# First batch of a gated recurrence: row maxima of chunks 0 and 1 spread from three 16-bit parts, and VectorE's scans placed ahead of a column copy

## The chip, the cores and the metric

One core of one Trainium2 chip. Its engines are TensorE (PE, with its weight loads PEld), VectorE (DVE), ScalarE (ACT), GpSimd (POOL) and SyncE (SP), which issues all transfers here. The metric is the time on the device in microseconds, as the median of several runs; beside it stands one execution taken by the hardware profiler.

## What is computed

Two blocks in a row. The first is a recurrence over 768 steps for 4 batches of 8 heads with 40 features:

```python
for t in range(S):
    m_new = np.maximum(f_gate[:, :, t] + m, i_gate[:, :, t])
    f_stab = np.exp(f_gate[:, :, t] + m - m_new)
    i_stab = np.exp(i_gate[:, :, t] - m_new)
    m = m_new
    C = f_stab * C + i_stab * outer(v_t, k_t)
    n = f_stab * n + i_stab * k_t
    y[:, :, t] = sigmoid(o_t) * (C @ q_t) / np.maximum(np.abs(n @ q_t), 1.0)
```

The second takes y as (4, 768, 320), adds the real part of its two-dimensional Fourier transform, normalizes each row, and adds a two-layer network with 1280 hidden features.

The running maximum m and the sum F of the forget gates are what matters here. In a chunk of 128 steps the weight of key s for query t is exp(a_s - M_t), where a is the input gate minus F, and M is the running maximum of a in that chunk's frame; keys later than the query are masked.

## The kernel before

All instructions stand in each engine's queue in the order in which the program emits them; a plan with slots and phases sets that order by hand. The first batch goes in 6 chunks of 128 steps, the other three in 12 half chunks. Batch 0 begins at once, in `gates()`, and everything of the other batches, the Fourier mix and the network follows in the plan.

In `gates()` rows are the 32 pairs of batch and head, columns are steps. For chunk 0 (`first`) and then for chunks 1 to 5 (`others`):

- `sums` (L205) scans the forget gates on VectorE into F; `maxima` subtracts F from the input gates (a, L210), copies the last F of each chunk (L212), scans the maxima into M (L213), and writes two small results, nM (L215) and m_in (L217).
- Chunk 0 goes backwards in time, so its maxima are copied in reverse into Mq, one element by ScalarE (L279), 127 by VectorE (L280).
- `columns(s, 0)` and `columns(s, 1)` (L273) turn a, and the keys' weights wk, into columns by TensorE transposes. Both land in one PSUM tile, `hb`, and are copied into colT (L282, L290, L296, L310). wk is written by ScalarE in `weights` (L263).
- `spread_max` makes, for four heads at a time, a PSUM tile pM that holds M along the columns in all 128 rows: one 16-bit product of an identity and a mask (L228) puts a large number where a key is later than the query, and one product per head (L233) adds that head's row of M. For chunks 0 and 1 the product is in float32: a column of the identity, repeated 128 times, times all 128 rows of M or Mq; this is why the rest of those rows is zeroed (L187, L188). For chunks 2 to 5 M is given as three bfloat16 parts, stacked in 96 rows (M3), and one 16-bit product with `sel` adds them up. `parts` (L239 to L243) makes the parts on GpSimd: round, subtract, round the rest, copy it, subtract again.
- `mlstm_exp` (L556) takes exp of column minus pM on ScalarE, `mlstm_scores` (L587) makes q times k, `mlstm_weigh` (L610) multiplies the two on VectorE, and two products (L587) follow: weights times values into `hb`, and keys times weighted values (vw, made by GpSimd, L574, from colT) into the new state `pc`.
- `spread_decay` (L258) spreads the queries' decay g (written by ScalarE in `decay`, L267) into pG, which VectorE multiplies with q into qg (L564).

PSUM is shared: pM, pG, pi and pc take turns on four banks. A product waits until what used the bank before has been read. `idle_products` (L143) are products of zeros whose result nobody reads.

After chunk 0's two halves of pM come the scores, then the five transposes of a, then pM of chunk 1, pG of chunk 1, the five transposes of wk, the scores of chunk 1, the products of chunk 0, and pM of chunk 2. VectorE, ahead of the subtraction at L210 for chunks 1 to 5, copies the second column of chunk 0 (L290), which waits for TensorE. Then it converts the first piece of the network's weights (L465, L467) between the second columns (L310) and the weighing of chunk 1. GpSimd sets several tiles to constants at its start (L189 to L199).

Of the kernel before, what the change touches and what calls it, by code (L numbers as in the profile page):

```python
# [10 lines left out]
FP = mybir.dt.float32  # L11
# [4 lines left out]
OP = mybir.AluOpType  # L16
PSUM = bass.MemoryType.PSUM

B, H, S, D = 4, 8, 768, 40
L = 128  # L20
NT = S // L
NP = H // 2
LH = L // 2
NS = S // LH
D1 = D + 1
BH = B * H
# [22 lines left out]
M_INIT = -1.0e30  # L49


def backwards(ap, start, n):

    return bass.AP(tensor=ap.tensor, offset=ap.offset + start, ap=[list(d) for d in ap.ap[:-1]] + [[-1, n]])
# [3 lines left out]
def kernel(  # L58
# [15 lines left out]
    nc = tc.nc  # L74
# [19 lines left out]
    def bank(name, shape, n=None):  # L94

        return ps_m.tile(shape, FP, name=name, tag=f"pm{next(turn) if n is None else n}")


    ident = const.tile([L, L], FP, name="ident")
# [3 lines left out]
    colT = const.tile([L, NT, 2, BH], FP, name="colT")  # L103
# [6 lines left out]
    alone = [const.tile([L, NP, LH], FP, name=f"alone{n}") for n in range(2)]  # L110
# [6 lines left out]
    states = [const.tile([L, NP * D1 + LH - D1], FP, name=f"C{n}") for n in range(6)]  # L117
# [22 lines left out]
    def idle_products(n, rest, at_=None):  # L140
        pw = bank("pi", [L, 2 * L], at_)
        for i in range(n):
            nc.tensor.matmul(pw, rest[:, 0:L], rest, start=True, stop=True, skip_group_check=True)  # L143


    def gates(gp):
        f_sb = gp.tile([BH, NT, L], FP, name="f_sb")
        a_flat = gp.tile([BH, S + 1], FP, name="a")
        a = a_flat[:, 0:S].rearrange("p (c t) -> p c t", t=L)
        rest = gp.tile([L, 2 * L], FP, name="rest")  # L150
# [3 lines left out]
        shift = gp.tile([BH, NT, L], FP, name="shift")  # L154
        m_in = gp.tile([BH, NT, 1], FP, name="m_in")
        F = gp.tile([BH, NT, L], FP, name="F")
        hT_bufs.extend(gp.tile([L, 4, L], FP, name=f"h{n}") for n in range(2))
        M, Mq = (gp.tile([L, NT, L], FP, name=name) for name in ("M", "Mq"))
        g, wk = (x_bufs[1].rearrange("p c m -> p (c m)")[0:n, i * S:(i + 1) * S].rearrange("p (c t) -> p c t", t=L)
                 for i, n in enumerate((L, BH)))  # L160
        nM = gp.tile([BH, NT], FP, name="nM")
        M3 = gp.tile([3 * BH, NT, L], BF, name="M3")
        below = gp.tile([BH, NT, L], BF, name="below")
        sel = gp.tile([3 * BH, BH], BF, name="sel")
# [19 lines left out]
        nc.vector.memset(keep, 1.0)  # L184
        nc.vector.memset(keep[:, :, 0:1], 0.0)
        nc.vector.memset(shift, 0.0)
        nc.vector.memset(Mq[:, 0], 0.0)  # L187
        nc.vector.memset(M[:, 1], 0.0)  # L188
        nc.gpsimd.memset(qk_bufs[1][:, 0], 0.0)  # L189
        mlstm_load_o(0, 0)  # L190
        mlstm_load(0, 1)
# [2 lines left out]
        nc.sync.dma_start(out=spread_sb, in_=spread)  # L194
        mlstm_load(0, 2)
        w1_pieces[1].load()
        for t in [t[:, NP * D1:] for t in states] + alone:
            nc.gpsimd.memset(t, 0.0)
        nc.gpsimd.memset(a_flat[:, S:], M_INIT)  # L199

        def flat(t, s):
            return t[0:BH, s].rearrange("p c t -> p (c t)")
# [5 lines left out]
        def maxima(s, initial):  # L208
            c0, c1 = s.start, s.stop
            nc.vector.tensor_tensor(out=a[:, s], in0=a[:, s], in1=F[:, s], op=OP.subtract)  # L210
            if c0 > 0:
                nc.vector.tensor_copy(out=shift[:, s, 0:1], in_=F[:, c0 - 1:c1 - 1, L - 1:L])  # L212
            nc.vector.tensor_tensor_scan(out=flat(M, s), data0=flat(shift, s), data1=flat(a, s), initial=initial,  # L213
                                         op0=OP.add, op1=OP.max)
            nc.vector.tensor_scalar(out=nM[:, s], in0=M[0:BH, s, L - 1], scalar1=-1.0, scalar2=None, op0=OP.mult)  # L215
            if c0 > 0:
                nc.vector.tensor_tensor(out=m_in[:, s], in0=M[0:BH, c0 - 1:c1 - 1, L - 1:L],  # L217
                                        in1=F[:, c0 - 1:c1 - 1, L - 1:L], op=OP.add)

        def spread_max(b, c, h0):  # L220

            k = chunks[b, c]
            if h0 == 0:
                k.W = wp.tile([L, H, L], FP, name="W", tag="W")
                k.M = []
            k.M.append(bank("pM", [L, NP, L], (0, 3)[h0 // NP] if c > 1 else None))
            later = later_r if c in BACKWARDS else later_b
            nc.tensor.matmul(k.M[-1], ident_b, later.unsqueeze(1).to_broadcast([L, NP, L]), start=True, stop=False,  # L228
                             skip_group_check=True)
            for h in range(h0, h0 + NP):  # L230
                bh = b * H + h
                w, x = (ident[:, bh:bh + 1], (Mq, M)[c][:, c, :]) if c < 2 else (sel[:, bh:bh + 1], M3[:, c, :])
                nc.tensor.matmul(k.M[-1][:, h - h0, :], w.to_broadcast([w.shape[0], L]), x, start=False, stop=True,  # L233
                                 skip_group_check=True)

        def parts(s):

            m, rest_ = (M if s.start == 2 else Mq)[0:BH, s], shift[:, s]
            nc.gpsimd.tensor_copy(out=M3[0:BH, s], in_=m)  # L239
            nc.gpsimd.tensor_tensor(out=rest_, in0=m, in1=M3[0:BH, s], op=OP.subtract)  # L240
            nc.gpsimd.tensor_copy(out=below[:, s], in_=rest_)
            nc.gpsimd.tensor_copy(out=M3[BH:2 * BH, s], in_=rest_)
            nc.gpsimd.tensor_tensor(out=M3[2 * BH:, s], in0=rest_, in1=below[:, s], op=OP.subtract)  # L243

        def queries():

# [14 lines left out]
        def weights(s):  # L261
            for c in range(s.start, s.stop):
                nc.scalar.activation(out=wk[:, c], in_=a[:, c], func=AF.Exp, bias=nM[:, c:c + 1])  # L263
# [6 lines left out]
        def columns(s, j):  # L270
            pt = first_heads_ps[:, j, 2 * L:2 * L + NT * BH].rearrange("p (c n) -> p c n", n=BH)
            for c in range(s.start, s.stop):
                nc.tensor.transpose(pt[:, c, :], (a, wk)[j][:, c, :], ident[0:BH, 0:BH])  # L273
            return pt

        first, others, last = slice(0, 1), slice(1, NT), slice(2, NT)
# [2 lines left out]
        nc.scalar.copy(out=Mq[0:BH, 0, 0:1], in_=M[0:BH, 0, 0:1])  # L279
        nc.vector.tensor_copy(out=Mq[0:BH, 0, 1:], in_=backwards(M[0:BH, 0], L - 1, L - 1))  # L280
        pt = columns(first, 0)
        nc.scalar.copy(out=colT[:, first, 0], in_=pt[:, first])  # L282
        weights(first)
        spread_max(0, 0, 0)
        pt = columns(first, 1)
        spread_max(0, 0, NP)
        mlstm_scores(0, 0)
        sums(others)
        mlstm_exp(0, 0, 0)
        nc.vector.tensor_copy(out=colT[:, first, 1], in_=pt[:, first])  # L290
        mlstm_exp(0, 0, NP)
        maxima(others, M[0:BH, 0, L - 1:L])
        pt = columns(others, 0)
        mlstm_load_o(0, 1)
        nc.vector.memset(g[:, 0:3], 0.0)
        nc.vector.tensor_copy(out=colT[:, others, 0], in_=pt[:, others])  # L296
        decay(slice(1, 2))
        weights(others)
        spread_max(0, 1, 0)
        spread_max(0, 1, NP)  # L300
        spread_decay(0, 1)
        pt = columns(others, 1)
# [30 lines left out]
        def gates_of_halves(step):  # L333
# [73 lines left out]
            else:  # L407
# [7 lines left out]
                if j == 0:  # L415
                    nc.scalar.copy(out=decB[:, NP:], in_=late["pd"][:, NP:])

        at(1, FILL + 0.2, parts, slice(2, 3))
        at(4, FILL - 0.45, queries)
        at(4, FILL + 0.2, parts, slice(3, NT))  # L420
        at(5, FILL_PE + 2.1, spread_decay, 0, 2)
        for c in range(2, NT):
# [85 lines left out]
    chunks = {}  # L508
# [37 lines left out]
    def mlstm_load_o(b, c):  # L546
        k = chunks[b, c]
        k.so = op_.tile([L, DM], FP, name="so", tag="so")
        nc.sync.dma_start(out=k.so, in_=o_gate[b, c])

    def mlstm_exp(b, c, h0):

        k = chunks[b, c]
        for h in range(h0, h0 + NP):
            M = k.M[h // NP][:, h % NP, :] if hasattr(k, "M") else k.W[:, h, :]
            nc.scalar.activation(out=k.W[:, h, :], in_=M, func=AF.Exp, scale=-1.0,  # L556
                                 bias=colT[:, c, 0, b * H + h:b * H + h + 1])
# [39 lines left out]
    def mlstm_scores(b, c):  # L597

        k = chunks[b, c]
        k.ps = [ps_s.tile([L, NP, L], FP, name=f"ps{hip}", tag="ps") for hip in range(2)]  # L600
        for p in range(NP):
            for hip, i in TILES:
                r = slice(hip * 64, hip * 64 + D)
                product(k.ps[hip][half(i), p, :], k.qk[r, 1, p, half(i)], k.qk[r, 0, p, :], True)
# [825 lines left out]
    hid.update({(0, r): mlp_p.tile([L, NFF // 2 * TG * L], FP, name=f"h0{r}") for r in range(2)})  # L1430
    gates_pool = ExitStack()
    gates(gates_pool.enter_context(tc.tile_pool(name="gates", bufs=1)))


# [212 lines left out]
```

## Time and profile before

| | us |
|---|---|
| median of 3 runs | 381.68 (380.98 to 381.75) |
| the profiled execution's own time | 382.09 |
| its span (first to last instruction) | 380.2 |
| PE busy in the span | 373.3 |
| DVE busy | 280.8 |
| ACT busy | 171.4 |
| POOL busy | 133.9 |

How to read it: the page gives busy shares and the span in 40 slices; the timeline gives instructions of an engine in order of time, neighbours of one kind merged into one row, with start, duration, count (a float32 product is two records), and in brackets the idle time before the row and who ended it. Neighbouring rows overlap a little, since engines are pipelined: the time from start to start is the pace. "Chain" is the path of waits followed back from the last instruction.

### The profile page before, as it was taken

How to read it: one execution, taken by the hardware profiler on the slowest of the kernel's cores; microseconds unless marked ns; L12 is line 12 of the kernel's file. 1: busy time of each engine (PE TensorE's matmuls, PEld its weight loads, DVE VectorE, ACT ScalarE, POOL GpSimd, SP SyncE). 2: the span in 40 equal slices, each digit the busy share in tenths (PEclk: the TensorE clock that was granted, in tenths of full speed). 3: DMA queues.
4: the chain of work that ended last, by engine and by line, in shares of the span. 5: the costliest groups of instructions: out<-in, count | busy, mean ns of one | idle time of the engine just before them, and what ended most of it. 6: DMA issues, size and time to landing. Idle time of an engine off the chain costs nothing.

```text
span 380.2 us, 11433 instructions
## 1 busy us (share of the span) xinstructions
PE 373.3 (98%) x4602; PEld 278.2 (73%) x4602; DVE 280.8 (74%) x662; ACT 171.4 (45%) x501; POOL 133.9 (35%) x240
## 2 busy tenths in 40 slices
PE   8999999999999999999999999999999999999996
PEld 6887655567677777666578999676488996546996
DVE  7788999999998585787964787987745885245552
ACT  4878757756442114764442153854520233544000
POOL 5568433775686124471501424561300000020000
PEclk9999999999999999999999999999999999999999
DMA  7978565999870428460002737300000001000011
GB/s 195 284 219 287 168 184 148 252 241 265 278 207 29 127 66 238 134 174 26 0 3 62 205 99 195 102 3 3 0 2 34 17 20 36 0 0 2 34 36 34
DMA packets 20500, 41.93 MB, mean 110 GB/s; under 512 B 3256, under 2 KB 9744, under 8 KB 20320
## 3 DMA queue, kind: packets, MB, share of 16 engines
q1 hardware_dynamic: 20448, 41.21, 37.5%
q8 instruction: 36, 0.59, 0.7%
q14 instruction: 16, 0.13, 0.1%
HBM read 37.10 MB, written 4.10 MB: 108 GB/s over the span
## 4 chain that ended last, share of the span: by engine, by line
PE 79%; DVE 9%; ACT 2%; issue 1%; SPq 1%; POOL 1%; DMA 0%; DVEq 0%; ACTq 0%; POOLq 0%
PE po L1346 22%; PE pm L1217 19%; PE po L1289 8%; PE pm L1134 7%; PE ph L587 5%; PE pm L1151 4%; PE ps L587 4%; PE pu L1004 3%; PE pz L958 2%; PE put L1053 2%; PE pzt L958 1%; PE hb L587 1%; DVE e L480 1%; DVE stats L1027 1%; DVE e L465 1%
## 5 line engine op out<-in xcount | busy, mean ns | idle before, releaser
L1295 DVE SCALAR_TENSOR_TENSOR x<-po,rstd,x 128x160 f32<-128x160 f32 (+1 forms) x69 | 27.1, 394 | 36.3 <-PE po L1346 33.0
L1223 DVE TENSOR_TENSOR h<-h,pm 128x384 f32<-128x384 f32 x60 | 30.5, 550 | 24.2 <-PE pm L1217 11.8
L583 POOL TENSOR_SCALAR_AFFINE_SELECT W<-W 64x512 f32<-64x512 f32 x36 | 28.1, 780 | 37.8 <-ACT W L556 28.8
L1217 PE MATMUL pm<-uT,w_sb 128*128 128x384 f32 x90 | 37.3, 503 | 0.1
L556 ACT ACTIVATE W<-W,colT 128x64 f32<-128x64 f32 x144 | 36.6, 336 | 1.6 <-DMA W<-M_d 1.6
L710 POOL TENSOR_TENSOR C<-C,decB 128x164 f32<-128x164 f32 x33 | 18.1, 549 | 49.4 <-DVE C L717 45.9
L1289 PE MATMUL po<-w_sb,h 128*128 128x320 f32 x120 | 33.6, 432 | 0.0
L1134 PE MATMUL pm<-uT,w_sb 64*64 64x384 f32 x320 | 32.0, 496 | 0.0
L1077 POOL TENSOR_TENSOR t<-rstd 128x6 f32<-128x6 f32 x12 | 3.7, 311 | 76.1 <-DVE v L1071 75.6
L568 POOL TENSOR_TENSOR qg<-qk,Gb 128x512 f32<-128x512 f32 x21 | 28.1, 1337 | 4.5 <-DMA Gb<-G_d 4.2
L1289 PEld LDWEIGHTS po<-w_sb,h 128*128 128x128 f32 x120 | 22.5, 190 | 8.9
L1151 PE MATMUL pm<-uT,w_sb 128*128 128x384 f32 x80 | 28.4, 496 | 0.0
L1346 PE MATMUL po<-T,S 128*128 128x160 f32 x180 | 27.8, 301 | 0.2 <-DVE x L1295 0.2
L1346 PEld LDWEIGHTS po<-T,S 128*128 128x128 f32 x180 | 25.4, 190 | 1.3 <-DVE x L1295 0.4
L1346 PE MATMUL po<-w_sb,h 128*128 128x160 f32 x180 | 26.3, 300 | 0.0
L1346 PEld LDWEIGHTS po<-w_sb,h 128*128 128x128 f32 x180 | 25.2, 190 | 1.4 <-DVE x L1295 0.3
L1217 PEld LDWEIGHTS pm<-uT,w_sb 128*128 128x128 f32 x90 | 15.7, 189 | 12.1 <-DVE h L1223 4.1
L1272 ACT ACTIVATE h<-h 128x384 f32<-128x384 f32 x45 | 23.1, 520 | 2.9 <-DVE h L1223 2.9
L1134 PEld LDWEIGHTS pm<-uT,w_sb 64*64 64x64 f32 x320 | 11.1, 132 | 15.5 <-issue 13.4
L574 POOL TENSOR_TENSOR vw<-kvt,colT 128x328 f32<-128x328 f32 x23 | 19.6, 852 | 7.0 <-DVE colT L290 2.7
L1151 PEld LDWEIGHTS pm<-uT,w_sb 128*128 128x128 f32 x80 | 14.3, 190 | 10.1 <-issue 1.2
L587 PE MATMUL ps<-qk 40*64 40x64 f32 (+1 forms) x768 | 19.9, 240 | 0.3 <-DVE C L717 0.3
(255 smaller groups left out, 825.2 us busy)
## 6 DMA issues: line engine op xcount, KB each, us to landing
kvt<-in_kv SPq DMA_DIRECT2D x24, 336.0 KB
qk<-in_qkT SPq DMA_DIRECT2D x48, 160.0 KB
raw<-in_w SPq DMA_DIRECT2D x10, 640.0 KB
W<-M_d SPq DMA_DIRECT2D x36, 128.0 KB
so<-in_o SPq DMA_DIRECT2D x24, 160.0 KB
out<-x SPq DMA_DIRECT2D x23, 160.0 KB
Gb<-G_d SPq DMA_DIRECT2D x42, 80.0 KB
ds_sb<-in_dft_s SPq DMA_DIRECT2D x1, 1158.0 KB
```

The lines of the kernel that those rows point to most:

```text
L556: nc.scalar.activation(out=k.W[:, h, :], in_=M, func=AF.Exp, scale=-1.0, bias=colT[:, c, 0, b * H + h:b * H + h + 1])
L568: nc.gpsimd.tensor_tensor(out=k.qg[:, :, t], in0=k.qk[:, 0, :, t], in1=k.Gb[:, :, t], op=OP.mult)
L583: nc.gpsimd.affine_select(out=W, in_=W, compare_op=OP.is_ge, fill=0.0, base=base, pattern=[[0, H], [-1 if back else 1, LH]], channel_multi ...
L587: nc.tensor.matmul(out, w, x, start=start, stop=True, skip_group_check=True)
L1134: nc.tensor.matmul(banks[i][half(cols)], w1_rest(n)[half(i), half(cols)], u[half(i)], start=start, stop=not start, skip_group_check=True)
L1151: nc.tensor.matmul(k.pm[i], w1_block(ch, f // 2 * 2 + i), u[2 * ch], start=(ch == 0 and not ahead), stop=(ch == 1 and (ahead or n in (2, 5 ...
L1217: nc.tensor.matmul(bank, w, u, start=start, stop=True, skip_group_check=True)
L1223: nc.vector.tensor_tensor(out=h, in0=h, in1=bank, op=OP.add)
L1272: nc.scalar.activation(out=h, in_=h, func=AF.Relu, scale=-1.0)
L1289: nc.tensor.matmul(k.po[m], hidden(gr, f)[:, i * L:(i + 1) * L], w2_sb[:, f, :], start=(f == 0), stop=(f == NFF - 1))
L1295: nc.vector.scalar_tensor_tensor(out=u, in0=po, scalar=k.rstd[:, c:c + 1], in1=u, op0=OP.mult, op1=OP.add)
L1346: nc.tensor.matmul(po, a[:, f], w[:, f], start=start and f == 0, stop=f == half - 1, skip_group_check=True)
```

## The change

- `spread_max` is split: `spread_mask` makes the mask's product, `spread_max` the heads' products. Chunk 0 has both masks made early, then one idle product on a bank of its own, then all eight heads' products together; the transpose of wk now follows these.
- Chunks 0 and 1 take the way of the other chunks: three 16-bit parts and one 16-bit product per head. Chunk 0's parts are made by GpSimd, one of the copies by ScalarE; chunk 1's parts are made by VectorE.
- M and Mq have 32 rows instead of 128, and the two memsets of VectorE that zeroed the rest are gone.
- On VectorE, the copy of chunk 0's second column stands after the scans for chunks 1 to 5 and after chunk 1's parts.
- Nine memsets of GpSimd stand after chunk 0's parts, and the memset of g goes from VectorE to GpSimd.

```diff
-        M, Mq = (gp.tile([L, NT, L], FP, name=name) for name in ("M", "Mq"))
+        M, Mq = (gp.tile([BH, NT, L], FP, name=name) for name in ("M", "Mq"))
...
-        nc.vector.memset(Mq[:, 0], 0.0)
-        nc.vector.memset(M[:, 1], 0.0)
...
-        for t in [t[:, NP * D1:] for t in states] + alone:
-            nc.gpsimd.memset(t, 0.0)
-        nc.gpsimd.memset(a_flat[:, S:], M_INIT)
...
-        def spread_max(b, c, h0):
+        def spread_mask(b, c, h0):
...
+        def spread_max(b, c, h0):
+
+            k = chunks[b, c]
+            if c > 0:
+                spread_mask(b, c, h0)
             for h in range(h0, h0 + NP):
-                bh = b * H + h
-                w, x = (ident[:, bh:bh + 1], (Mq, M)[c][:, c, :]) if c < 2 else (sel[:, bh:bh + 1], M3[:, c, :])
-                nc.tensor.matmul(k.M[-1][:, h - h0, :], w.to_broadcast([w.shape[0], L]), x, start=False, stop=True,
-                                 skip_group_check=True)
-
-        def parts(s):
-
-            m, rest_ = (M if s.start == 2 else Mq)[0:BH, s], shift[:, s]
-            nc.gpsimd.tensor_copy(out=M3[0:BH, s], in_=m)
-            nc.gpsimd.tensor_tensor(out=rest_, in0=m, in1=M3[0:BH, s], op=OP.subtract)
-            nc.gpsimd.tensor_copy(out=below[:, s], in_=rest_)
-            nc.gpsimd.tensor_copy(out=M3[BH:2 * BH, s], in_=rest_)
-            nc.gpsimd.tensor_tensor(out=M3[2 * BH:, s], in0=rest_, in1=below[:, s], op=OP.subtract)
+                w = sel[:, b * H + h:b * H + h + 1]
+                nc.tensor.matmul(k.M[h0 // NP][:, h - h0, :], w.to_broadcast([w.shape[0], L]), M3[:, c, :], start=False,
+                                 stop=True, skip_group_check=True)
+
+        def parts(s, eng=nc.gpsimd):
+
+            m, rest_ = (M if s.start in (1, 2) else Mq)[0:BH, s], shift[:, s]
+            eng.tensor_copy(out=M3[0:BH, s], in_=m)
+            eng.tensor_tensor(out=rest_, in0=m, in1=M3[0:BH, s], op=OP.subtract)
+            eng.tensor_copy(out=below[:, s], in_=rest_)
+            (nc.scalar.copy if s.start == 0 else eng.tensor_copy)(out=M3[BH:2 * BH, s], in_=rest_)
+            eng.tensor_tensor(out=M3[2 * BH:, s], in0=rest_, in1=below[:, s], op=OP.subtract)
...
         pt = columns(first, 0)
+        spread_mask(0, 0, 0)
+        spread_mask(0, 0, NP)
+        idle_products(1, rest, 0)
         nc.scalar.copy(out=colT[:, first, 0], in_=pt[:, first])
         weights(first)
+        parts(first)
+        for t in [t[:, NP * D1:] for t in states] + alone:
+            nc.gpsimd.memset(t, 0.0)
+        nc.gpsimd.memset(a_flat[:, S:], M_INIT)
+        nc.gpsimd.memset(g[:, 0:3], 0.0)
         spread_max(0, 0, 0)
+        spread_max(0, 0, NP)
         pt = columns(first, 1)
-        spread_max(0, 0, NP)
         mlstm_scores(0, 0)
         sums(others)
         mlstm_exp(0, 0, 0)
-        nc.vector.tensor_copy(out=colT[:, first, 1], in_=pt[:, first])
         mlstm_exp(0, 0, NP)
         maxima(others, M[0:BH, 0, L - 1:L])
+        parts(slice(1, 2), nc.vector)
+        nc.vector.tensor_copy(out=colT[:, first, 1], in_=pt[:, first])
         pt = columns(others, 0)
         mlstm_load_o(0, 1)
-        nc.vector.memset(g[:, 0:3], 0.0)
```

## The prediction

> **What bounds the kernel now.** I read the page's busy shares, then the timeline of the first 20 us engine by engine, then the chain that ended last. The page:
>
> ```profile
> PE 373.3 (98%) x4602; PEld 278.2 (73%) x4602; DVE 280.8 (74%) x662; ACT 171.4 (45%) x501; POOL 133.9 (35%) x240
> PEclk9999999999999999999999999999999999999999
> ```
>
> TensorE (PE) is occupied all the time, so a change at the start is worth what it moves PE's later work forward. The clock row does not help before 10.83 us: the trace's record of the granted clock has its first entry there. Rows show the clock instead. PE's timeline:
>
> ```profile
> 4.34 0.61 PE L228 MATMUL pM<-later_r,ident_b 128*128 128x512 bf16 x1
> 4.97 2.04 PE L233 MATMUL pM<-Mq,ident 128*128 128x128 f32 x8
> 6.95 0.31 PE L273 MATMUL hb<-ident,x 32*128 32x32 f32 x1
> 7.59 1.91 PE L233 MATMUL pM<-Mq,ident 128*128 128x128 f32 x8
> 9.43 1.76 PE L587 MATMUL ps<-qk 40*64 40x128 f32 x32
> 11.12 0.49 PE L273 MATMUL hb<-ident,a 32*128 32x32 f32 x5
> 11.77 1.05 PE L233 MATMUL pM<-M,ident 128*128 128x128 f32 x8
> 13.86 1.09 PE L258 MATMUL pG<-x,ident 128*64 128x128 f32 x16
> 14.88 0.49 PE L273 MATMUL hb<-ident,x 32*128 32x32 f32 x5
> 18.04 0.39 PE L233 MATMUL pM<-M,sel 96*128 96x128 bf16 x4
> 18.27 0.38 PE L228 MATMUL pM<-later_b,ident_b 128*128 128x512 bf16 x1
> 19.26 1.09 PE L258 MATMUL pG<-x,ident 128*64 128x128 f32 x16 [0.39 <-DVE dec L320]
> ```
>
> Columns: start, duration, engine and line, out<-in, count, idle time before. Four float products of the maxima (8 records) take 1.98 us start to start at 4.97 (to 6.95), and 0.89 us at 11.77 (the next mask starts at 12.66): the same work at half and at full clock. Four products of 16-bit parts take 0.23 us at 18.04 (to 18.27). VectorE (DVE) and GpSimd (POOL):
>
> ```profile
> 4.41 0.42 DVE L280 COPY Mq<-M 32x127 f32<-32x127 f32 x1
> 4.54 1.47 DVE L205 TENSOR_TENSOR_SCAN F<-keep,f_sb 32x640 f32<-32x640 f32 x1
> 7.29 0.19 DVE L290 COPY colT<-hb 128x32 f32<-128x32 f32 x1 [1.29 <-PE hb L273]
> 7.40 0.80 DVE L210 TENSOR_TENSOR a<-a,F 32x640 f32<-32x640 f32 x1
> 8.13 0.69 DVE L212 COPY shift<-F 32x5 f32<-32x5 f32 x1
> 8.86 1.54 DVE L213 TENSOR_TENSOR_SCAN M<-shift,M,a 32x640 f32<-32x640 f32 x1
> 15.42 0.33 DVE L310 COPY colT<-hb 128x160 f32<-128x160 f32 x1 [2.25 <-PE hb L273]
> 7.57 1.23 POOL L574 TENSOR_TENSOR vw<-kvt,colT 128x328 f32<-128x328 f32 x1 [2.71 <-DVE colT L290]
> 12.02 0.42 POOL L243 TENSOR_TENSOR M<-shift,below 32x128 bf16<-32x128 f32 x1
> ```
>
> VectorE idles 1.29 us for a column copy before the scans of chunks 1 to 5, and 2.25 us at 15.42 for PE's second transposes. From that copy (15.42) on VectorE is full: conversion, weighing, copy of the state, qg to 19.1, and PE's row at 19.26 waits for VectorE. **So the sum goes by one number: when PE's five transposes that end at 15.31 end.** From 19 us the chain of waits passes through PE, VectorE, ScalarE, GpSimd and a few loads in turn until 77.8, then lies on PE almost to the end; I found no release in it that is fixed in time, so what is won at 15.31 I carry to the end whole.
>
> **The change, part by part.**
>
> *Chunk 0.* Removed: eight float products, 1.98 + 1.84 us on PE at half clock (4.97 to 6.95, 7.59 to 9.43). Added: eight 16-bit products. No row shows them at half clock; bounds 0.23 per four (full-clock row) and 0.51 (that times 1.98/0.89); I take 0.45, so 0.9 in all, since the rows around run at half clock. They wait for the parts: Mq is written at 4.83, then four GpSimd steps at the start-to-start times of the same steps at 10.47: 0.36 + 0.48 + 0.37 + 0.42 = 1.6, to 6.5. ScalarE's fifth part (about 0.2) lies beside them, after its exp of the keys' weights (ends 4.93). PE meanwhile does both masks (from 4.34, about 0.85) and one idle product (0.98, a third of the 2.93 of the first row): to 6.2, then idle 0.3. Products 6.55 to 7.45, a transpose 0.24, scores 7.7 to 9.45: 1.7 earlier than 9.43 to 11.12. The two exps' halves end at 9.4 instead of 10.68. The two VectorE memsets removed (0.17 each) give nothing: the next subtraction waits for the load of the input gates, which lands at 3.48 in the trace.
>
> *Chunks 1 to 5.* The column copy no longer stands ahead: a minus F starts at 6.05 instead of 7.40. Its small copy (8.13) took 0.69 beside GpSimd's vw; bounds 0.2 (the 32x5 rows at 10.5 take 0.16 and 0.25) and 0.69, or longer if GpSimd's moved memsets hold it; I take 0.4. Then the scan 1.54 and two small steps 0.4: 9.2. Now five part steps of 32x128 on VectorE; no such row. Nearest: VectorE's 32x128 subtraction, 0.28 (0.32 start to start), and GpSimd's whole set, 1.97 (10.47 to 12.44). Bounds 0.9 and 1.97; I take 1.15, by the VectorE row. So the parts of chunk 1 are there at 10.3 and the column copy (0.19) ends at 10.5. The memset of g (0.38) goes to GpSimd, where it ends about 8.1, ahead of ScalarE's decay at 9.4.
>
> *The new wait.* PE's five transposes of a write the PSUM tile that the column copy reads, and in the built program they wait for that copy; before, the copy was long done. Behind them in PE's queue stand masks, products, pG, the second transposes and the next scores. So PE idles from 9.45 to 10.5, and 1.05 of the 1.7 won is given back. vw on GpSimd also waits for the copy (10.5 instead of 7.5), with the parts of chunk 2 behind it: 10.55 + 0.95 + 1.97 = 13.5, needed by PE not before about 17: hidden; if not, PE would wait there.
>
> *From 10.5 to the second transposes.* Before: 11.12 to 15.31, 4.19 us. After, at full clock: transposes 0.42, two masks and eight products 0.9, pG 1.02, transposes 0.43 = 2.8, ending at 13.3: 2.0 us won. At half clock: 0.5 + 1.75 + 1.9 + 0.5 = 4.65, ending at 15.15: 0.15 won. **Which clock PE has decides.** Before, PE ran on without a break from 4.97, and from 7.19 without transposes, until the clock rose at 10.83: 5.9 or 3.6 us. After, it pauses 0.3 us at 6.2 and 1.05 us at 9.45, so I let the stretch start anew at 10.5: the rise comes at 14.1 to 16.4. I take 14.2, since the 3.6 is the one of a stretch like this. Then transposes and products end at 12.75, pG has 1.45 of its 1.9 behind it at 14.2 and ends at 14.45, the transposes at 14.85: **0.45 us won**; with the later rise 0.15. ScalarE's exps of chunk 1 end near 14.2 instead of 15.1 and do not bind.
>
> [...]
>
> **Sum.** The profiled execution took 382.09 (span 380.2), 0.41 above the median 381.68. 382.09 - 0.45 = 381.6 for an execution like it; against the median 381.68 - 0.45 = 381.2. About 0.2% (0.76 us) is what a measurement can tell from no change.
>
> **Rivals.**
> 1. *Clock up early.* The stretch from 1.24 to 6.2 (three idle products, masks, one more) is 4.9 us, longer than 3.6, and may raise the clock before the pauses; or the pauses do not count. For it: PE is occupied in it. Against: 1.24 to 7.4 in the trace of before was as full and did not raise it. Then 2.0 us won: 379.7.
> 2. *VectorE late, slower.* Its small copy at 6.8 meets GpSimd's moved memsets (6.5 to 8.1); at 8.13 in before such a copy ended with GpSimd's vw. Held to 8.1 it adds 1.0, and parts at GpSimd's price 0.8: the column copy ends at 12.3, PE's second transposes at about 16.6 (3.6 at half clock, then 0.65): 1.25 lost, 382.9. It is a loss once the copy ends after about 11.05. Against: each memset is short (0.06 to 0.4), and a copy could slip in between.
> 3. *Clock up very late,* after 16.4: scores and the products behind them run at half clock too; 0.15 won turns into 0 to 0.5 lost: 381.7 to 382.2.
> 4. *Nothing of it arrives:* a load or GpSimd holds the middle stretch. Nothing in the chain speaks for it; it falls into the forecast's lower end.
>
> **Numbers.** Forecast 48% (won 0.1 to 1.1: 380.6 to 381.6; a third of it beyond 0.2%), rival 1 25%, rival 2 15%, rival 3 12%. Faster 0.17 + 0.25 = 0.42; slower 0.15 + 0.05 = 0.20; same 0.38. The range takes in rival 1 and most of rival 2: 379.5 to 382.6; the forecast's own is 380.6 to 381.6.
>
> **What would show it.** Scores of chunk 0 at about 7.7; PE idle about 1 us before the five transposes at 10.5, released by VectorE; five VectorE steps summing to 1.15; eight products of chunk 1 taking 0.45 per four (half clock) or 0.23; the second transposes at 14.4 instead of 14.88; pG of chunk 2 at 18.8 instead of 19.26. If the products of chunk 1 run at 0.23 per four, rival 1 holds; if the small copy lasts until GpSimd's memsets end, rival 2.

## The result, and the profile after

| | before | after |
|---|---|---|
| median beside each other, 14 runs each | 380.94 (379.27 to 382.28) | 385.82 (382.33 to 392.92) |
| ratio, 95% interval | | 1.0101 [1.0068, 1.0133] |
| the profiled execution's own time | 382.09 | 387.49 |
| its span | 380.2 | 385.4 |
| chunk 0's scores start (PE) | 9.43 | 10.32 |
| second transposes start | 14.88 | 16.63 |
| pG of chunk 2 starts | 19.26 | 23.26 |

The kernel after is 1% slower; the prediction was 381.2, with a range that ended at 382.6. (Executions over 1.5% above the fastest of their kernel, three of the 14 of after, are left out of every ratio; the ranges in brackets hold them.) Busy shares and clock row of the page of after:

```profile
PE 374.9 (97%) x4588; PEld 278.6 (72%) x4588; DVE 282.7 (73%) x664; ACT 171.7 (45%) x502; POOL 137.5 (36%) x245
PEclk9589999999999999999999999999999999999999
```

PE has 14 matmuls less than before, yet the clock row has a hole in its second and third slice (9.6 to 28.9 us), where that of before has none. PE's timeline of after (start, duration, line, out<-in, count, idle time before and its releaser):

```profile
5.17 0.81 PE L143 MATMUL pi<-rest 128*128 128x256 f32 x2
9.13 1.01 PE L233 MATMUL pM<-M,sel 96*128 96x128 bf16 x8 [3.16 <-POOL M L243]
...
10.32 1.99 PE L595 MATMUL ps<-qk 40*64 40x128 f32 x32
12.24 0.74 PE L273 MATMUL hb<-ident,a 32*128 32x32 f32 x5
...
16.63 0.74 PE L273 MATMUL hb<-ident,x 32*128 32x32 f32 x5
...
23.26 1.09 PE L258 MATMUL pG<-x,ident 128*64 128x128 f32 x16
```

PE pauses for 3.16 us before chunk 0's products, released by GpSimd's last part step, and what follows runs at half speed until 22.66: the transposes of a take 0.74 instead of 0.49. The clock records of this execution say the same: full from 5.59 to 9.00, half from 9.00 to 22.66. The windows view (a stretch and its length, then the busy time and number of instructions of PE, PEld, DVE, ACT, POOL, then the granted clock, the DMA share and GB/s) has both halves of it in two rows:

```profile
6.00:8.00 2.00, 0.00 (x0) 0.10 (x1) 1.93 (x4) 0.30 (x1) 1.77 (x4) 1.00 0.86 240
...
10.00:12.00 2.00, 2.00 (x35) 1.76 (x33) 1.27 (x6) 2.00 (x9) 0.94 (x4) 0.50 1.07 325
```

From 6 to 8 us PE does nothing while VectorE (1.93) and GpSimd (1.77) are both full; from 10 on PE is full at clock 0.50. Why GpSimd needs so long is in the timelines of these two, laid side by side:

```profile
4.57 1.47 DVE L200 TENSOR_TENSOR_SCAN F<-keep,f_sb 32x640 f32<-32x640 f32 x1
6.07 0.81 DVE L205 TENSOR_TENSOR a<-a,F 32x640 f32<-32x640 f32 x1
6.81 0.38 DVE L207 COPY shift<-F 32x5 f32<-32x5 f32 x1
7.23 1.63 DVE L208 TENSOR_TENSOR_SCAN M<-shift,M,a 32x640 f32<-32x640 f32 x1
...
9.10 0.98 DVE L239 CAST M<-M 32x128 bf16<-32x128 f32 x1
...
11.24 0.19 DVE L301 COPY colT<-hb 128x32 f32<-128x32 f32 x1
```

```profile
4.78 1.34 POOL L239 CAST M<-Mq 32x128 bf16<-32x128 f32 x1 [0.86 <-DVE Mq L280]
6.21 0.96 POOL L240 TENSOR_TENSOR shift<-Mq,M 32x128 f32<-32x128 f32 x1
7.24 0.28 POOL L241 CAST below<-shift 32x128 bf16<-32x128 f32 x1
7.60 1.49 POOL L243 TENSOR_TENSOR M<-shift,below 32x128 bf16<-32x128 f32 x1
```

Three of GpSimd's four steps took 1.34, 0.96 and 1.49 us; the same steps at 10.47 in before took 0.28, 0.42 and 0.42. Add start and duration in each list: the VectorE scan ends at 6.04 and GpSimd's cast at 6.12; subtraction and small copy end at 6.88 and 7.19, GpSimd's subtraction at 7.17; the second scan ends at 8.86, GpSimd's last step at 9.09. The parts are ready at 9.1, not at 6.5.

There is a second loss, much later. In the waits view of after (who waited for whom: total, times, longest), beside the 3.2 us stand stretches that nothing in the profile releases:

```profile
PE pM L233 <- POOL M L243: 3.2, 1, 3.2
PE ph L595 <- issue: 1.9, 2, 1.3
```

They are at 90.4 and 98.3 us (1.31 and 0.62). In before the only such stretch is one of 0.43 at 147.3. So the profiled execution lost 4.0 us by 23 us and 1.5 more in these stretches, less 0.3 that is not accounted for: 5.2, its difference in span.

### The profile page after: what moved, and what is told of

It reads as the page before. It is cut to its first block, busy times and chain, and to the rows that moved or that the text cites. A ratio compares the mean times of both kernels' runs of the same rounds, so it can differ in the third digit from the quotient of the medians.

```text
span 385.4 us, 11412 instructions
## 1 busy us (share of the span) xinstructions
PE 374.9 (97%) x4588; PEld 278.6 (72%) x4588; DVE 282.7 (73%) x664; ACT 171.7 (45%) x502; POOL 137.5 (36%) x245
## 4 chain that ended last, share of the span: by engine, by line
PE 86%; DVE 7%; POOL 2%; issue 2%; ACT 2%; DMA 1%; DVEq 0%; POOLq 0%; ACTq 0%
PE po L1354 22%; PE pm L1225 19%; PE po L1297 8%; PE pm L1142 7%; PE ph L595 5%; PE ps L595 5%; PE pm L1159 4%; PE pu L1012 3%; PE pz L966 2%; PE put L1061 2%; PE hb L595 2%; PE pzt L966 1%; PE pz L978 1%; DVE stats L1035 1%; DVE e L488 1%
## 5 line engine op out<-in xcount | busy, mean ns | idle before, releaser
L576 POOL TENSOR_TENSOR qg<-qk,Gb 128x512 f32<-128x512 f32 x21 | 27.0, 1287 | 7.1 <-DMA Gb<-G_d 6.7
L595 PE MATMUL ps<-qk 40*64 40x64 f32 (+1 forms) x768 | 21.0, 247 | 0.3 <-DVE C L725 0.3
```

The source lines that it names most:

```text
L576: nc.gpsimd.tensor_tensor(out=k.qg[:, :, t], in0=k.qk[:, 0, :, t], in1=k.Gb[:, :, t], op=OP.mult)
L595: nc.tensor.matmul(out, w, x, start=start, stop=True, skip_group_check=True)
```

## The experiments

Three theories stood at the start. **T1:** VectorE's scans slow GpSimd's parts, PE pauses for 3 us, and the pause throws the clock to half. **T2:** the pause costs by itself, the clock is only a companion. **T3:** the order costs, since PE's transposes of a now wait for a copy that stands behind the scans. A yardstick for all of them is the start of pG of chunk 2, where the start of the kernel ends. The ratios are each against the kernel before, on the same chip.

### Order alone (T3)

```diff
-        nc.vector.tensor_copy(out=colT[:, first, 1], in_=pt[:, first])
         mlstm_exp(0, 0, NP)
         maxima(others, M[0:BH, 0, L - 1:L])
+        nc.vector.tensor_copy(out=colT[:, first, 1], in_=pt[:, first])
```

> The kernel before, with float32 products and all memsets as they were; only the column copy of chunk 0 stands after VectorE's scans. Theory 1 (the loss comes from chunk 0's parts): no pause of PE, maxima of chunk 1 at about 9 instead of 10.4, nothing waits for them: within 0.2% of before, at most 0.5 us faster. Theory 3 (the wait for the copy costs): PE idles ahead of the transposes of a and the kernel is about 1 us slower than before.

Measured: 380.23, ratio 0.9986 [0.9963, 1.0008]; pG of chunk 2 at 17.53, clock up at 7.05. **T3 falls:** the order costs nothing. It was run again later, beside others:

> The kernel before with only the column copy moved behind the scans, unchanged from the earlier run of it, to stand beside the two others on one chip: 380.2 us as before, ratio 0.996 to 1.001. If that order is worth something, the interval's upper end stays below 1.000; if not, it includes 1.000.

380.38, 0.9993 [0.9957, 1.0029], pG at 17.04. Both intervals include 1: the head start of 1.4 us (a minus F at 6.02 instead of 7.40) is not worth anything that can be measured either. With the clock up by 4 to 7 us, 17.0 to 17.5 is the place of pG against which a late start has to be counted; the 19.26 of the trace of before belongs to an execution whose clock rose only at 10.83.

### Chunk 0 in float32, the rest of the change kept

Edit: Mq has 128 rows again with its memset; the early `spread_mask`, the idle product and `parts(first)` of chunk 0 go; the transpose of wk stands between the halves of pM as before; and `spread_max(0, 0, ...)` takes `ident` and Mq as before; chunk 1's parts on VectorE and the late copy stay.

> Chunk 0 as before the change (float32 products, mask and products in the old order); chunk 1 as after it (16-bit parts by VectorE, scans ahead of the column copy, memset of g on GpSimd). Theory 1 (GpSimd's parts of chunk 0 are slowed by VectorE's scans, PE stands still 3.2 us, and the clock falls for it): no pause of PE at 6 us, no fall of the clock, column copy at about 10.6, PE's transposes of a still at 11.1, products of chunk 1 cheaper by 1.4 us at full clock: 1 to 1.5 us faster than before, about 379.6, with a spread like that of before. Theory 2 (the pause alone costs, the clock would be low anyhow): the same sign, 0 to 1 us faster. Theory 3 (the wait for the column copy is what costs): this kernel keeps it, so PE still idles about 1 us ahead of the transposes of a and it is 1 us or more slower than before.

382.79, ratio 1.0015 [0.9983, 1.0047]: no loss, but no gain of 1 us or more either, so the number expected was missed. The wait on the copy that the prediction had added is there (PE's timeline of this run):

```profile
10.37 0.49 PE L275 MATMUL hb<-ident,a 32*128 32x32 f32 x5 [1.20 <-DVE colT L299]
```

VectorE's five part steps, with no GpSimd beside them, take 0.21, 0.28, 0.21, 0.22 and 0.28. The clock rose at 6.32, and pG of chunk 2 started at 17.56, where the order alone has it at 17.53. So in these two executions the 16-bit products for chunk 1 win nothing with the clock up: the wait of 1.20 takes nearly all that they give, and the 0.35 us by which PE still stood ready sooner (16.79 against 17.14) went in VectorE's conversion, which took 0.86 instead of 0.48.

The reverse, chunk 0 as in after and chunk 1 in float32 (M has 128 rows again with its memset):

```diff
+                w, x = (ident[:, bh:bh + 1], M[:, c, :]) if c == 1 else (sel[:, bh:bh + 1], M3[:, c, :])
...
-        parts(slice(1, 2), nc.vector)
```

> Chunk 0 as after the change (parts by GpSimd), chunk 1 in float32 as before, copy after the scans. Theory 1: the pause of 3.2 us and the fall of the clock are all there: 385 to 387 with a wide spread; the float32 products cost 1 to 2 us more but load PE more. Theory 3 (parts of chunk 1 ahead of the copy are the cost): the copy ends at 9.4, nothing waits, so 381 to 382.

386.55, ratio 1.0139 [1.0089, 1.0188], and PE's pause is there again, with clock up at 4.25, down at 7.67, back at 17.91:

```profile
9.16 1.01 PE L236 MATMUL pM<-M,sel 96*128 96x128 bf16 x8 [3.80 <-POOL M L246]
```

**The loss is chunk 0's part of the change.**

### Why the parts are late

Parts of chunk 0 with the scans held: a one-element VectorE copy of the last part stands ahead of the scans, so that no scan runs beside GpSimd.

```diff
         mlstm_scores(0, 0)
+        nc.vector.tensor_copy(out=warm[64:65, 3:4], in_=M3[64:65, 0, 0:1])
         sums(others)
```

> As after the change, but one more tiny VectorE copy reads chunk 0's finished parts ahead of the long scans, so that no scan runs beside GpSimd's part steps. Theory 1: the four GpSimd steps take 1.5 to 1.7 us instead of 4.3 (casts 0.28, subtractions 0.42), parts there at about 6.4; scans start 1.9 us later, and the pause moves to the transposes of a. If instead GpSimd is slow for another reason (these steps are slow at first use, or the loads hold SBUF), its steps still take about 4 us and the parts come at 9.

GpSimd's timeline of this run:

```profile
4.74 0.28 POOL L239 CAST M<-Mq 32x128 bf16<-32x128 f32 x1 [0.83 <-ACT colT L285]
5.11 0.42 POOL L240 TENSOR_TENSOR shift<-Mq,M 32x128 f32<-32x128 f32 x1
5.59 0.28 POOL L241 CAST below<-shift 32x128 bf16<-32x128 f32 x1
5.95 0.42 POOL L243 TENSOR_TENSOR M<-shift,below 32x128 bf16<-32x128 f32 x1
```

The four steps take 1.63 us from 4.74 to 6.37 instead of 4.31, on the same data in the same place: **that the scans beside them slow them is shown** (a later run with the scans held, below, has the same four durations). Three of the four steps of after each end 0.08 to 0.29 us behind a VectorE scan or subtraction of 640 columns that ran beside them (6.12 behind 6.04, 7.17 behind 6.88, 9.09 behind 8.86); one does not: the cast at 7.24 took its undisturbed 0.28 beside a scan that had started at 7.23, and here the scan was the longer one, 1.63 instead of the 1.54 that it takes with GpSimd quiet. By what means they slow each other is not shown.

The time did not come back: 385.64, 1.0101 [1.0063, 1.0139]. The pause had only moved. With the scans late, the column copy is late, and PE's transposes of a wait:

```profile
6.42 0.61 PE L233 MATMUL pM<-M,sel 96*128 96x128 bf16 x8 [0.81 <-POOL M L243]
...
12.34 0.73 PE L273 MATMUL hb<-ident,a 32*128 32x32 f32 x5 [4.11 <-DVE colT L302]
```

The same with the parts of chunk 0 made by VectorE, ahead of its scans (`parts(first, nc.vector)`):

> As after the change, but chunk 0's parts are made by VectorE ahead of its scans, not by GpSimd. [...] Theory 2: the sum of the pauses is somewhat smaller, 382 to 383 with a spread like that of before. Theory 3: the wait is longer than after the change, so slower than after it, 386 or more.

384.74, 1.0101 [1.0074, 1.0129]. PE's first pause is 0.22, its second, for the copy, 3.84; the clock was up at 5.77, down at 9.18, back at 16.01. In these three versions, whoever makes chunk 0's parts, PE has nothing to do for 3 to 5 us: the pauses add up to 3.2 in after, 4.9 with the scans held and 4.1 here.

### Is it the clock, or the pause? (T1 against T2)

Five idle products instead of one in the first pause, which they nearly fill (0.51 is left):

```diff
-        idle_products(1, rest, 0)
+        idle_products(5, rest, 0)
```

> As after the change, but five idle products instead of one fill the pause of PE (0.4 us each at full clock, 0.9 at half). Theory 1: the pause shrinks to 0 to 1.4 us, the clock does not fall in most executions, so 381 to 383 and a spread of 3 us instead of 10. Theory 2: the parts still come at 9.1, so nothing is won: 385 to 386 with the same spread.

GpSimd's steps are as slow as in after (1.34, 0.96, 0.28 and 1.49), and the products start at 9.02. But in the profiled execution the clock rose at 7.22 and stayed, and pG of chunk 2 started 1.0 us (0.3%) behind 17.53:

```profile
18.55 1.09 PE L258 MATMUL pG<-x,ident 128*64 128x128 f32 x16 [0.75 <-DVE dec L328]
```

The time was 383.17, ratio 1.0037 [1.0001, 1.0074]. The spread was 11 us, not 3 as expected: five of the twelve executions still had a mean clock of 0.986 or 0.996. With both pauses filled (nine products in the first, three more ahead of the transposes of a):

> As after the change, but nine idle products instead of one in the first pause and three ahead of the transposes of a, so that PE has something to do in both pauses. Theory 1 (pauses bring the clock down; the late parts alone cost little): hardly any execution with a clock below 1.00 after its first rise, median 381 to 382.5, most executions within 3 us. Theory 2 (the parts that come at 9.1 are the cost, not the clock): 385 to 386 as after the change, or more, since idle products at half clock (0.9 us each) stand ahead of the real ones.

382.52, 1.0049 [1.0023, 1.0075], all executions with a mean clock of 0.999 or 1.0; pG at 19.46. That is 1.9 us later than 17.53, which is 0.5% of 380 us. But 0.9 of it, compared with the run before, is the filling's own: VectorE's copy ended at 11.34, and the three added idle products kept PE from the transposes of a until 12.65:

```profile
11.16 1.56 PE L143 MATMUL pi<-rest 128*128 128x256 f32 x6
12.65 0.49 PE L273 MATMUL hb<-ident,a 32*128 32x32 f32 x5
```

**With the clock held, the late parts move the end of the start by 1.0 us (0.3%), and the ratios of 1.0037 and 1.0049 against 1.0101 leave half or more of the loss to the fallen clock.** The intervals touch (1.0074 and 1.0075 above, 1.0068 below), so the division is rough; T1 and T2 each hold in part. The eleven executions of after in the ratio fit only partly: four with a mean clock of 0.981 or 0.982 took 385.1 to 387.5 and one at 0.987 388.05, but four at 0.991 took 382.3 to 384.9, no more than two at 1.0 with 382.9 and 384.4. This mean counts the time ahead of the first clock record as full (before's trace has 0.999 with its first record at 10.83), so a late first rise does not show in it.

Held scans and both pauses filled (three products in the first, eight in the second):

> The kernel after with both losses taken away: VectorE's scans held until GpSimd's parts of chunk 0 are made (GpSimd then needs 1.6 us, as with the scans held alone), three idle products instead of one in TensorE's first pause and eight (about 3.9 us at full clock) in its second, so that the clock stays up from about 5 us on. If the stretched parts and the fallen clock are the whole cause, pG of chunk 2 starts at 19.3 to 20.3 (the scans are later by the hold, and the transposes of a start at about 12.3 and take 2.8 us to the second transposes), and the ratio to before is 1.000 to 1.004. If something else of the change costs as well (the 16-bit parts, the order), it is 1.008 or more with a clock of 1.0 throughout.

383.61, 1.0056 [1.0021, 1.0090]. pG at 19.55, as expected, and again about 2.0 us (0.5%) behind 17.53; the expectation of 1.000 to 1.004 had counted from the 19.26 of before's trace, and so from the wrong clock. Its profiled execution, the slowest of the twelve (386.92), has something else, a stretch of 3.00 us that nothing releases (PE's timeline):

```profile
86.98 0.34 PE L597 MATMUL ph<-kvt,W 64*64 64x41 f32 x8
90.32 0.56 PE L597 MATMUL ph<-kvt,W 64*64 64x41 f32 x23 [3.00 <-issue]
```

The clock was down from 91.63 to 95.04, right behind it.

### The stretches that nothing releases

They came up with the chunk 0 in float32 version, when two idle products were put ahead of its transposes of a to fill the 1.20 us there:

```diff
+        idle_products(2, rest, 0)
         pt = columns(others, 0)
```

> Chunk 0 in float32 as before, chunk 1 by 16-bit parts of VectorE (as in the first experiment), with two idle products in PE's pause ahead of the transposes of a. Theory 1: the first experiment lost its 1.4 us to executions in which this pause let the clock down; with the pause filled the median falls from 382.8 to about 380 to 381, spread as before. If the cheap 16-bit products themselves are what keeps the clock low (they load the array less), the median stays at 382 to 383.

382.91, 1.0056 [1.0028, 1.0083], not the 380 to 381 expected, though in the profiled execution (385.17) the clock stayed up from 6.02 on and pG of chunk 2 stood at 17.51. The time goes later, by the waits view:

```profile
PE ph L594 <- issue: 2.5, 3, 1.2
PE put L1060 <- issue: 2.3, 1, 2.3
```

The trace has 36 transfers on a queue of instructions (the page's q8, 0.59 MB in all, so 16 KB each). Beside each of the longer stretches lies one: in this run one at 147.9 to 149.0 with PE stopped from 148.4 to 150.7; in the run above one at 87.6 to 88.8 with PE stopped from 87.3 to 90.3; in after one at 89.1 to 90.4 and PE stopped from 90.4 to 91.75. In every such stretch of 0.4 us or more, in all the profiles, PE goes on 1.3 to 1.7 us after a transfer has landed. Most fall into or right behind half chunks in which PE goes through over a hundred matmuls of 64x41 or 40x64 (in the run above 104 in 1.6 us). So PE seems to run out of instructions there, which these transfers suggest and no record shows, and whether it does may depend on what was put in front. First, two products of one column on the order-alone kernel:

```diff
+        for i in range(2):
+            nc.tensor.matmul(pw[:, 0:1], rest[:, 0:L], rest[:, 0:1], start=True, stop=True, skip_group_check=True)
         pt = columns(others, 0)
```

> The kernel before with only the column copy moved behind the scans, plus two one-column products of zeros ahead of the transposes of a (four more instructions on TensorE, some 0.1 us each). By their own time: at most 0.4 us, ratio to the same kernel without them 1.000 to 1.001 (about 380.2 to 380.6 us). If the stretches that TensorE loses later without a wait (0.7 to 2.4 us beside transfers of instructions, seen in the runs with two idle products) depend on where in the instruction stream the kernel stands, the profile shows such stretches of over 0.5 us at other places, and the time moves by 1 us or more.

380.55, 0.9999 [0.9955, 1.0043], longest such stretch 0.2 us: four more instructions cost nothing that can be measured. Then more of them, on the order-alone kernel, with the three idle products of the start cut into twelve of 64 columns:

> The kernel before with only the column copy moved behind the scans; its three idle products of 256 columns at the start are cut into twelve of 64: the same columns in the same stretch of 2.9 us, but 18 more matmuls ahead of everything else on TensorE. If the position in the instruction stream does nothing: 380.2 to 380.6 us, ratio 0.997 to 1.002. If the extra instructions of the idle products are what costs the versions with a steady clock their remaining 0.5%, the ratio is 1.003 or more, and the profile shows stretches of over 0.5 us in which TensorE waits for nothing that the profile shows, at 85 to 92 us.

388.03, 1.0196 [1.0155, 1.0236]. Its profile has two such stretches, 2.29 at 79.5 us and 1.38 at 109.4. But the twelve took 5.38 us instead of 2.93 (0.22 a record, where a quarter of the columns would make it 0.12), so the start was 2.5 us late as well, and the run does not tell the two apart. The next one does better: one product of 512 columns and nine of 32x32 with one column.

> The kernel before with only the column copy moved behind the scans; its three idle products at the start become one of 512 columns (two thirds of their time) and nine of 32x32 with one column (18 small instructions): 14 more instructions on TensorE in about the same 2.9 us. By their time alone: ratio 0.997 to 1.002, 380.2 to 381.0 us. If instructions ahead of the dense stretch cost, 1.005 or more, with stretches of over 0.5 us at 75 to 92 us in which TensorE waits for nothing that the profile shows.

```profile
3.24 1.12 PE L173 MATMUL pi<-rest 32*32 32x1 f32 x18
4.29 0.31 PE L276 MATMUL hb<-ident,a 32*128 32x32 f32 x1
...
18.63 1.09 PE L261 MATMUL pG<-x,ident 128*64 128x128 f32 x16 [0.39 <-DVE dec L323]
...
77.30 0.38 PE L590 MATMUL ph<-C,qg 40*64 40x41 f32 x12 [0.96 <-issue]
...
81.33 2.93 PE L1154 MATMUL pm<-uT,w_sb 128*128 128x384 f32 x4 [1.81 <-issue]
```

The 18 small ones take 1.12 us, and the first transpose is 0.2 us late (4.29 instead of 4.10). The clock rose only at 9.55, so that pG of chunk 2 is 1.1 us behind 17.53; whether the small products delayed the rise is not shown (in before's trace it came at 10.83 without them). The time is 385.71, 1.0141 [1.0086, 1.0197]. 2.8 us are lost in two such stretches, and the clock was down from 81.24 to 84.65 behind the second; all six executions had a mean clock of 0.990 to 0.996. In the 35 executions of before beside the first runs seven had 0.995 or 0.996, and these took 382.7 to 385.3, the others 379.2 to 382.9. **Fourteen more small instructions at the start, on a kernel with no pause, cost 1.4%, in the profile mostly between 76 and 85 us.**

### Chunk 0 alone, with the clock held

Chunk 0 as in after, chunk 1 in float32, nine idle products in the first pause and one ahead of the transposes of a:

> Chunk 0 as in the kernel after (parts by GpSimd beside VectorE's scans), chunk 1 in float32 as before, and nine idle products instead of one in the first pause, one more ahead of the transposes of a, so that the clock stays up. The ratio of this version without idle products was 1.0139. If the fallen clock is the larger part of that: ratio 1.000 to 1.006 with a clock of 0.999 to 1.0 in every execution, and pG of chunk 2 at 18.5 to 20 instead of 22.98. If the clock were only a companion of the late parts, the ratio stays at 1.010 or more.

385.61, 1.0135 [1.0097, 1.0172]. At 20 us it had won what was expected (pG 19.53 instead of 22.98), in the median nothing: by itself this run speaks for T2. Its profiled execution has 1.5 us of stretches that nothing releases, and three of its six executions had a clock of 0.995 or 0.996. So the idle products that hold the clock have a price of the kind just seen. With fewer, wider ones (five of 512 columns instead of nine of 256):

> Chunk 0 as in the kernel after, chunk 1 in float32, the first pause filled by five products of 512 columns instead of nine of 256 (8 fewer instructions, some 4606 instead of 4614). By the instruction count: ratio 1.000 to 1.006 where the other had 1.0135. If the count is nothing and chunk 0's parts cost by themselves with the clock held, 1.010 or more again.

384.14, 1.0078 [1.0048, 1.0107], no such stretch in its profile, pG at 19.61. That lies between the two expectations and decides neither. And the version with both pauses filled, by five and two wide products:

> The kernel after with its two pauses filled as in the run with nine and three idle products, but by five and two products of 512 columns: about the same time of TensorE, 8 fewer instructions on it (some 4602 instead of 4610, as many as in the kernel before). If the number of instructions ahead of the dense stretch of small products at 75 to 92 us is what costs those 0.5%, the ratio is 0.998 to 1.003 with a clock of 1.0. If it is the late parts themselves, it stays at 1.003 to 1.007.

384.32, 1.0074 [1.0044, 1.0104], above both expectations. The count does not explain this one: it has 4600 matmuls, fewer than before, and no gain over the 1.0049 with 4610. Its wide products overrun both pauses (pG at 20.28, 0.8 later), and its profile has stretches of 1.57 and 0.41 all the same.

## Why the prediction was wrong

**The step that failed** is the first: "four GpSimd steps at the start-to-start times of the same steps at 10.47: 0.36 + 0.48 + 0.37 + 0.42 = 1.6, to 6.5". Beside the rows at 10.47 VectorE had two small steps, a memset and a copy from PSUM, and from 11.89 a product with one factor in PSUM; after the move, two scans and a subtraction of 640 columns stand exactly beside these steps. Measured 4.3, to 9.1; with the scans held 1.63, so the price was right for an idle neighbour. The first scan stood at 4.54 in the prediction's own rows, the prediction itself moved the subtraction ("a minus F starts at 6.05") and the second scan into that window, and it never set the two timelines side by side. The term "idle 0.3" became 3.16.

**The clock, second.** The prediction let the half-speed stretch "start anew" at a pause and took no fall from full speed. Here the clock was up at 5.59, before the pause, and fell at 9.00 until 22.66. The early rise is the condition of rival 1 (25%, 2.0 us won); that the clock could fall again is in none of the rivals. Rival 3, "Clock up very late" (12%), had the half speed after 16.4, but priced it at 0 to 0.5 lost, since PE was thought to be late by nothing else.

**The new wait** on the column copy was right as a mechanism: 1.20 in the run with chunk 0 in float32 (predicted 1.05). In after it is hidden, because PE comes to it late. Its size follows the parts: 3.84 and 4.11 where these stand ahead of the scans.

**The five VectorE steps,** 1.15 predicted: 1.33 from first start to last end (8.75 to 10.08) where nothing disturbs them, within the bounds. In after the first took 0.98 beside GpSimd's memsets (9.14 to 10.45), the others 0.21 to 0.28; the copy ended at 11.43, not 10.5. That is what the rival "VectorE late" expected beside GpSimd's memsets, at another instruction.

**Right:** the small copy 0.38 (predicted 0.4), a minus F at 6.07 (6.05), four products at half clock 0.42 from start to start (0.45). The copy was luck: it takes 0.15 with GpSimd quiet, and what stood beside it was GpSimd's subtraction, not the memsets. None of the three decided anything.

**"What is won at 15.31 I carry to the end whole"** held for losses only in part: 4.0 us at 23 us are in the span whole, but 1.5 us more came from stretches that the trace of before gave little sign of (one of 0.43). And the yardstick was off: before's profiled execution (382.09, 1.15 above the median of 380.94) had its clock up at 10.83, while in the order-alone kernel's two profiled executions it rose at 7.05 and 4.38. A gain that consists of fewer slow products shrinks when the clock is up sooner: chunk 1's 16-bit products won nothing there (17.56 against 17.53).

**What stays open.** How the 1.0% divides in a typical execution: the runs with the clock held leave 0.4 to 0.7% with chunk 1 in 16 bits, but 0.8 and 1.4% with chunk 1 in float32, and they carry idle products with a price of their own. What exactly sets the stretches without a releaser: that instructions put in front can bring them is shown by one pair of kernels, that PE waits for its instruction stream is argued from the transfers beside them, and the number of instructions alone does not order the versions (4600 matmuls 1.0074, 4606 0.9999 and 1.0078, 4610 1.0049, 4616 1.0141). No version tried is measurably faster than before.

## What to carry to other kernels

Before a step is moved to another engine, lay the two engines' timelines over each other as they will be after all moves: a duration from a row with an idle neighbour need not hold beside a busy one, as here the cast of 0.28 that took 1.34 beside a scan. On the engine that is full to the end, first ask whether the change opens a pause of some microseconds; here pauses of 3 to 4 us were followed by 7 to 14 us at half clock, and the products that the change was to save were 3.8 us. And a change of a few instructions at the start of a long stream can cost about 1% at a far place, as the kernel with the small products did (1.0141): look for stretches without a releaser before a loss is put down to the edit.

## What the runs showed of the hardware

- VectorE scans and subtractions of 32x640 beside GpSimd stretched its 32x128 cast from 0.28 to 1.34, and its subtractions from 0.42 to 0.96 and 1.49; a second cast beside a scan stayed at 0.28. GpSimd's memsets stretched a VectorE cast from 0.21 to 0.98.
- In pauses of PE of 3.16, 3.84 and 3.80 us (after, parts by VectorE, chunk 1 in float32) the clock fell to half 3.0, 1.1 and 2.3 us from their beginning, and it came back 13.7, 6.8 and 10.2 us later. With the parts by VectorE PE was busy from 11.95 on and the clock was back at 16.01, 4.1 us later; in after PE was busy from 9.13 on and the clock came back at 22.66, 13.5 us later. In the clock records of after these stretches are multiples of 3.41 (3.41 up, four times 3.41 down); what sets them is not shown.
- Ahead of the clock's rise a float32 product took 0.49 per record with 256 columns (2.93 for six), 0.25 with 128 (1.98 for eight) and 0.22 with 64 (5.38 for 24): going from 128 to 64 columns saved little there. One with 32x32 weights and one column took 0.06.
- Stretches of 0.4 to 3.0 us in which PE waits for nothing visible, ending 1.3 to 1.7 us after a 16 KB transfer of instructions had landed; those of 1.81 (small products), 1.83 (scans held), 2.29 (twelve products) and 3.00 (scans held, pauses filled) were followed by one stretch of 3.41 us at half clock, that of 2.35 (chunk 0 in float32 with idle products) was not. In steps of 3.41 from each trace's first rise, the four left PE idle for 1.7 to 2.3 us of one step, while the 2.35 lay across the end of one (1.0 and 1.3 us). Idle time alone does not tell them apart: 1.57 us within one step (wide products in both pauses) brought no fall, and with the parts by VectorE the clock fell after 1.3.
